# The bias row of a fused recurrence and MLP kernel: a matmul of ones against block transposes and a round trip through DRAM

## The chip, the cores and the metric

The kernel runs on one core of a Trainium2 chip. The metric is device time in microseconds (us); lower is better. The core's engines work side by side, each through its own list of instructions in order: TensorE (PE, with its weight loads shown as PEld), VectorE (DVE), ScalarE (ACT), GpSimd (POOL), and SyncE (SP), which here only issues DMAs. An instruction that waits for another engine or for a DMA holds everything behind it on its own engine.

## The reference

Two stages, joined. The first is a gated linear recurrence over 768 steps for 4 batches and 8 heads of width 48; its output is laid out as 3072 tokens of 384. The second is an MLP with a squared ReLU, a scale s and a bias b:

```
for t in range(S):
    state = alpha[:, :, t, :, None] * state + k[:, :, t] (x) v[:, :, t]
    y[:, :, t] = q[:, :, t] . state
x = y as [3072, 384]
r = max(x @ w_in, 0)              # w_in: 384 x 2048
g = s * (r * r) + b
out = g @ w_out                   # w_out: 2048 x 384
```

Since b is a single number, `g @ w_out` is `(r * r) @ (s * w_out)` plus one row that is the same for every token: b times the sum of each column of w_out. That row of 384 numbers is the **bias row**. The change is about how it is made.

## The kernel before, in words

The 3072 tokens are cut into 24 units of 128 (six units, n % 6 = 0 to 5, make one batch). For each unit the recurrence is done in chunk form. ACT takes the logarithm of alpha (`ln`, L239), PE sums it along the chunk (`cum_pe`, L255), ACT makes the two exponentials (`cum_act`, L268 and L269), DVE multiplies k and q by them (`kb_mul` L317, `qb_mul` L320), PE transposes both (`tr`, L328), and DVE copies the transposes to SBUF (`qk_copy`, L340). PE multiplies them into scores (`amat`, L361), DVE masks the scores (`mask`, L370), and PE makes the unit's output from scores and carried state (`y_pe`, L466 and L475). The state goes on through `t1` (DVE, L549) and `sd` (POOL, L559 and L563). The result is transposed for the MLP (`xt_pe` L527, `xt_act` L534). The MLP of a unit is four pieces u = 0 to 3: PE multiplies by w_in (`mp`, L573, 12 matmuls of 128 columns for each of four blocks, taken together by the trace), ACT applies the ReLU (`rl`, L586), DVE squares (`sq`, L593), PE multiplies by w_out (`o_pe`, L604). The sum of all four pieces stands in one bank of PSUM, `o_ps`.

Two places hold results back. Outputs of units 0 to 13 are parked in SBUF (`keep_sb`, which lies over the spent tile `w_in_st`); DVE adds the bias row to them later (`add_bias`, L655) and SP stores them. From unit 14 on, DVE adds the row while it empties `o_ps` (`o_out`, L621).

The bias row before is made so: DVE adds the sixteen 128-row blocks of the fp32 w_out (`w_out_st`) into `cs_sb` in seven additions of two blocks (`colsum`, L201 and L203), then one more (`bias_sum`, L206). Now `cs_sb[:, 0]` holds 128 partial sums for each of the 384 columns. `bias_row` multiplies a matrix of ones by it on PE, in fp32, into the PSUM bank `y_ps` (L209). That sums over the 128 partitions and puts the same row on all of them. ACT scales it by b into `bias_w` (L210).

The order of work is written out by hand. Each step is put at a position (`at(pos, ...)`), the list is sorted by position, and each engine gets its instructions in that order. From unit 10 on positions repeat with a period of 16 for two units, an even and an odd one, which take about 13.86 us, so one position is about 0.87 us. SP's DMAs go into one queue in the same order: for unit n a row of decays out to DRAM (`row_dr`, L304), the loads of unit n + 3 (L132), and the decays back, one number for each partition (`blast`, L311). SP waits for a semaphore before it issues a DMA, and the DMAs share eight completion semaphores in turn: the ninth DMA waits until the first has landed.

Names that the steps below use: `w_out_st` (the fp32 copy of w_out, no longer read once the column sums are done), `cs_sb`, `bias_w`, `y_ps`, `qkT` (the SBUF copy of the transposes), `sb_col` (s and b on every partition).

Of the kernel before, what the change touches and what calls it, by code (L numbers as in the profile page):

```python
# [8 lines left out]
FP32 = mybir.dt.float32  # L9
BF16 = mybir.dt.bfloat16  # L10
AF = mybir.ActivationFunctionType
ALU = mybir.AluOpType

@with_exitstack
def kernel(
# [12 lines left out]
    nc = tc.nc  # L28
# [6 lines left out]
    d_model = moe_w_in.shape[0]  # L35
# [13 lines left out]
    sb = ctx.enter_context(tc.tile_pool(name="sb", bufs=1))  # L49
    ps = ctx.enter_context(tc.tile_pool(name="ps", bufs=1, space=bass.MemoryType.PSUM))  # L50
    dr = ctx.enter_context(tc.tile_pool(name="dr", bufs=1, space=bass.MemoryType.DRAM))
# [5 lines left out]
    y_ps = ps.tile([128, 512], FP32, name="y_ps")  # L57
# [6 lines left out]
    def ring(name, shape, dtype, n):  # L64
        return [sb.tile(shape, dtype, name=f"{name}{i}") for i in range(n)]
# [12 lines left out]
    ones_f = sb.tile([128, 128], FP32, name="ones_f")  # L78
    sb_row = sb.tile([1, 2], FP32, name="sb_row")
    sb_col = sb.tile([128, 2], FP32, name="sb_col")  # L80
    s_col, b_col = sb_col[:, 0:1], sb_col[:, 1:2]
# [18 lines left out]
    qkT_p = qkT_all.rearrange("a u y -> a (u y)").rearrange("a (x p b s i) -> a x p b s i", x=2, p=NP, b=2, s=2)  # L100
    am_sb = [ring("am_a", [128, NP, 128], BF16, 2), ring("am_b", [128, NP, 128], BF16, 2)]
    blast = ring("blast", [128, NP, 1], FP32, 3)
    row_dr = [dr.tile([1, H * 48], FP32, name=f"row_dr{i}") for i in range(3)]
    t1_sb = sb.tile([128, NP, 96], FP32, name="t1_sb")
    sc_sb = sb.tile([128, NP, 96], FP32, name="sc_sb")
# [10 lines left out]
    w_out_st = sb.tile([128, NJ, d_model], FP32, name="w_out_st")  # L116
    w_out_bf = sb.tile([128, NJ, d_model], BF16, name="w_out_bf")
    cs_sb = sb.tile([128, 2, d_model], FP32, name="cs_sb")
    bias_w = sb.tile([128, d_model], FP32, name="bias_w")


    NKEEP = 14
# [82 lines left out]
    def bias_sum():  # L205
        nc.vector.tensor_tensor(out=cs_sb[:, 0], in0=cs_sb[:, 0], in1=cs_sb[:, 1], op=ALU.add)  # L206

    def bias_row():
        nc.tensor.matmul(out=y_ps[:, 0:384], lhsT=ones_f, rhs=cs_sb[:, 0], start=True, stop=True)  # L209
        nc.scalar.activation(out=bias_w, in_=y_ps[:, 0:384], func=AF.Copy, scale=b_col)  # L210

    def spread():
        nc.tensor.matmul(out=p_ps[:, 510:512], lhsT=ones_f[0:1], rhs=sb_row, start=True, stop=True)
# [286 lines left out]
    h0, h1, o, ct, a0, a1 = h_ps[0], h_ps[1], o_ps, ct_ps, *(a.rearrange("a p t -> a (p t)") for a in a_ps)  # L500
# [202 lines left out]
    for s in range(2):  # L703
        nc.vector.memset(mask_p[s], 0.0)
        for b in range(2):
            part = mask_p[s][64 * b : 64 * b + 64]
            nc.gpsimd.affine_select(
                out=part,
                in_=part,
# [17 lines left out]
    def at(pos, fn, *args):  # L727
        events.append((pos, len(events), fn, args))
# [55 lines left out]
    for i in range(3, 8):  # L784
        at(69.3 + 8 * (i - 3), colsum, i)
    at(103.3, bias_sum)
    at(105.5, bias_row)
    for n in range(NKEEP):
        at(125.3 + 4.55 * n, add_bias, n)
        at(126.2 + 4.55 * n, store, n, keep_sb[n])  # L790
# [15 lines left out]
    for n in range(4, NBLK):  # L806
        p = 8 * n
        f = max(0.0, min((n - 5) / 3.0, 1.0))
        c, t, a = 9.0 + 5.8 * f, 5.8 + 5.0 * f, 3.4 + 4.5 * f
# [59 lines left out]
```

## Time and profile before

| | us |
|---|---|
| three timed runs: median (lowest to highest) | 187.06 (186.27 to 187.86) |
| the execution that was profiled: its time | 185.68 |
| its span, first to last instruction | 183.9 |
| TensorE busy | 177.7 (97%) |
| VectorE busy | 143.4 (78%) |
| ScalarE busy | 122.6 (67%) |
| GpSimd busy | 60.3 (33%) |
| DMA data moved | 30.33 MB, mean 165 GB/s |

The profile is one execution. Its time is its span and 1.78 us around it, and it lies 1.38 us under the median of the timed runs. Busy times are sums of one engine's instructions over the whole span. TensorE's clock was granted in full throughout (1.000). Where the text says "at 119.14", it is the time in us from the start of the span. "Idle before, releaser" names what ended an engine's wait. Starts of matmuls in the timeline lie some tenths earlier than in the chain, since matmuls are pipelined.

### The profile page before, as it was taken

How to read it: one execution, taken by the hardware profiler on the slowest of the kernel's cores; microseconds unless marked ns; L12 is line 12 of the kernel's file. 1: busy time of each engine (PE TensorE's matmuls, PEld its weight loads, DVE VectorE, ACT ScalarE, POOL GpSimd, SP SyncE). 2: the span in 40 equal slices, each digit the busy share in tenths (PEclk: the TensorE clock that was granted, in tenths of full speed). 3: DMA queues.
4: the chain of work that ended last, by engine and by line, in shares of the span. 5: the costliest groups of instructions: out<-in, count | busy, mean ns of one | idle time of the engine just before them, and what ended most of it. 6: DMA issues, size and time to landing. Idle time of an engine off the chain costs nothing.

```text
span 183.9 us, 6223 instructions
## 1 busy us (share of the span) xinstructions
PE 177.7 (97%) x2506; PEld 142.3 (77%) x2506; DVE 143.4 (78%) x301; ACT 122.6 (67%) x253; POOL 60.3 (33%) x97
## 2 busy tenths in 40 slices
PE   7998999999999999999999999999999999999993
PEld 2565899866698687787888778878878878878793
DVE  7699879666657688987898976699789799886541
ACT  3888797985678956656766766846746746734750
POOL 7436471113230725042505343143103343333000
PEclk9999999999999999999999999999999999999999
DMA  6999999999188989982975564936895942214212
GB/s 156 315 324 359 235 295 385 255 213 207 16 166 169 188 173 177 172 174 41 169 140 121 105 125 92 192 63 145 171 201 139 211 133 92 73 59 157 60 52 77
DMA packets 105263, 30.33 MB, mean 165 GB/s; under 512 B 98436, under 2 KB 103699, under 8 KB 105235
## 3 DMA queue, kind: packets, MB, share of 16 engines
q1 hardware_dynamic: 105230, 29.94, 70.1%
q8 instruction: 19, 0.31, 0.7%
q14 instruction: 10, 0.07, 0.1%
q10 hardware_dynamic: 4, 0.00, 0.0%
HBM read 25.19 MB, written 4.74 MB: 163 GB/s over the span
## 4 chain that ended last, share of the span: by engine, by line
PE 90%; ACT 4%; DVE 3%; issue 1%; POOL 1%; ACTq 0%; POOLq 0%; DVEq 0%
PE h_ps L573 29%; PE o_ps L604 28%; PE ct_ps L328 5%; PE h_ps L604 3%; PE a_ps L573 2%; PE a_ps L361 2%; PE o_ps L229 2%; PE y_ps L475 2%; PE ct_ps L573 2%; PE h_ps L527 2%; PE ct_ps L255 2%; PE o_ps L573 2%; PE y_ps L466 1%; PE a_ps L630 1%; PE a_ps L604 1%; PE p_ps L488 1%
## 5 line engine op out<-in xcount | busy, mean ns | idle before, releaser
L573 PEld LDWEIGHTS <-w_in_bf 128*128 128x128 bf16 x1152 | 67.5, 98 | 5.1 <-DVE w_in_bf L176 0.9
L586 ACT ACTIVATE r_sb<-h_ps 128x512 bf16<-128x512 f32 x79 | 46.9, 603 | 30.7 <-PE h_ps L573 28.9
L604 PE MATMUL o_ps<-w_out_bf,gt_all 128*128 128x384 bf16 x320 | 64.0, 326 | 0.0
L573 PE MATMUL h_ps<-xd_all,w_in_bf 128*128 128x128 bf16 x948 | 60.3, 219 | 0.0
L559 POOL TENSOR_TENSOR sd_sb<-t_sb,blast 48x192 bf16<-48x192 f32 x40 | 26.9, 672 | 85.8 <-DVE t_sb L549 57.8
L593 DVE TENSOR_TENSOR gt_all<-r_sb 128x512 bf16<-128x512 bf16 x96 | 40.8, 442 | 16.5 <-ACT r_sb L586 16.3
L604 PEld LDWEIGHTS <-gt_all 128*128 128x128 bf16 x368 | 32.5, 98 | 15.6 <-issue 0.2
L250 POOL CAST v_bf<-v_sb 128x384 bf16<-128x384 f32 x23 | 15.4, 678 | 21.2 <-DMA v_sb<-in_v_dram 19.2
L317 DVE TENSOR_TENSOR kb_sb<-k_sb,bi_sb 128x384 bf16<-128x384 f32 x24 | 14.3, 595 | 7.1 <-ACT bi_sb L268 7.1
L534 ACT ACTIVATE xd_all<-h_ps 128x384 bf16<-128x384 bf16 x19 | 9.5, 502 | 8.6 <-PE h_ps L527 8.6
L320 DVE TENSOR_TENSOR qb_sb<-q_sb,b_sb 128x384 bf16<-128x384 f32 x24 | 13.5, 565 | 1.6 <-ACT b_sb L269 1.6
L563 POOL TENSOR_TENSOR sc_sb<-t_sb,blast 112x384 f32<-112x384 f32 x16 | 13.8, 864 | 1.3
L239 ACT ACTIVATE la_sb<-al_sb 128x384 bf16<-128x384 f32 x24 | 12.5, 529 | 2.6 <-DVE blast L720 2.3
L497 ACT ACTIVATE y_bf<-y_ps 128x384 bf16<-128x384 f32 x22 | 10.9, 497 | 3.5 <-PE y_ps L475 3.1
L340 DVE COPY qkT<-ct_ps 112x1024 bf16<-112x1024 bf16 x16 | 11.0, 686 | 2.3 <-PE ct_ps L328 2.1
L370 DVE TENSOR_TENSOR am_a<-a_ps,mask 128x512 bf16<-128x512 f32 x13 | 8.9, 688 | 4.4 <-PE a_ps L361 4.2
L328 PEld LDWEIGHTS <-qb_sb 128*112 128x112 bf16 x96 | 8.1, 130 | 3.4 <-DVE qb_sb L320 1.9
L268 ACT ACTIVATE bi_sb<-ct_ps 128x384 f32<-128x384 f32 x19 | 9.3, 489 | 2.1 <-PE ct_ps L255 1.9
L370 DVE TENSOR_TENSOR am_b<-a_ps,mask 128x512 bf16<-128x512 f32 x13 | 8.9, 684 | 1.7 <-PE a_ps L361 1.7
L269 ACT ACTIVATE b_sb<-ct_ps 128x384 f32<-128x384 f32 x19 | 9.4, 495 | 0.0
L655 DVE TENSOR_TENSOR w_in_st<-w_in_st,bias_w 128x384 f32<-128x384 f32 x14 | 8.3, 595 | 0.0
L328 PEld LDWEIGHTS <-kb_sb 128*112 128x112 bf16 x96 | 7.2, 130 | 0.7 <-DVE kb_sb L317 0.4
(142 smaller groups left out, 254.8 us busy)
## 6 DMA issues: line engine op xcount, KB each, us to landing
al_sb<-in_alpha_dram SPq DMA_DIRECT2D x20, 192.0 KB, 2.7
q_sb<-in_q_dram SPq DMA_DIRECT2D x20, 192.0 KB, 4.3
k_sb<-in_k_dram SPq DMA_DIRECT2D x20, 192.0 KB, 7.2
v_sb<-in_v_dram SPq DMA_DIRECT2D x20, 192.0 KB, 3.6
w_in_st<-in_moe_w_in_dram SPq DMA_DIRECT2D x4, 768.0 KB
w_out_st<-in_moe_w_out_dram SPq DMA_DIRECT2D x4, 768.0 KB
out_dram<-w_in_st SPq DMA_DIRECT2D x10, 192.0 KB
out_dram<-out_sb SPq DMA_DIRECT2D x5, 192.0 KB, 2.0
```

The costliest lines, as they stand in the source:

```text
L239: nc.scalar.activation(out=la_sb[n % 2][:, :, 0:48], in_=raw("al", n), func=AF.Ln)
L250: nc.gpsimd.tensor_copy(out=v_bf[n % 4], in_=raw("v", n))
L317: nc.vector.tensor_tensor(out=kb_sb[n % 4][:, :, 0:48], in0=raw("k", n), in1=bi_sb[n % 2], op=ALU.mult)
L320: nc.vector.tensor_tensor(out=qb_sb[n % 2][:, :, 0:48], in0=raw("q", n), in1=b_sb[n % 3], op=ALU.mult)
L328: nc.tensor.transpose(out=t_bank(n, x if n in pair_of else None)[0:112, x, p, :], in_=t.rearrange("a h d -> a (h d)")[:, 128 * p : 128 * p ...
L370: nc.vector.tensor_tensor(out=am_sb[e][n % 2], in0=a_bank(n)[e], in1=mask4, op=ALU.mult)
L559: nc.gpsimd.tensor_tensor(out=sd[r, :, d], in0=t1_sb[r, :, d], in1=bl[r].to_broadcast([48, NP, 48]), op=ALU.mult)
L563: nc.gpsimd.tensor_tensor(out=sc_sb[0:112], in0=t1_sb[0:112], in1=bl[0:112].to_broadcast([112, NP, 96]), op=ALU.mult)
L573: nc.tensor.matmul(out=hp[:, jj * C : (jj + 1) * C], lhsT=w_in_bf[:, kk, 128 * j : 128 * (j + 1)], rhs=xd_sb[n][:, kk], start=(kk == 0), s ...
L586: nc.scalar.activation(out=rs, in_=room((g, u)), func=AF.Relu)
L593: nc.vector.tensor_tensor(out=gt_sb[g][:, u * 512 : (u + 1) * 512], in0=rs, in1=rs, op=ALU.mult)
L604: nc.tensor.matmul(out=op[:, 0:d_model], lhsT=gt_sb[n][:, j * C : (j + 1) * C], rhs=w_out_bf[:, j, :], start=(j == 0), stop=(j == NJ - 1),)
```

## The change

The matmul of ones and the scaling on ACT are taken out. In their place:

- `bias_turn` (position 110.0), on DVE: `cs_sb[:, 0]` is transposed in blocks of 32 x 32 into `cs_sb[:, 1]`; then each partition of a group of 32 holds, for 12 columns of w_out, 32 partial sums side by side. A reduction sums each 32, so `part_sb` gets 12 numbers for each partition, and these are multiplied by b. Each of the four groups of 32 partitions now holds one partial bias row, scattered as 32 x 12.
- `bias_spread` (position 110.4), on SP: four small DMAs write the four partial rows to DRAM in the order of columns, 384 numbers of 4 bytes each; a fifth reads the four rows (6,144 bytes) back onto every one of the 128 partitions, into the first four blocks of `w_out_st` (786,432 bytes in all).
- `bias_add` (positions 120.5 and 123.5), on DVE: two additions make one row of the four, `bias_w`.

The additions of the bias to the parked outputs stay at positions 125.3 and on.

```diff
-    def bias_row():
-        nc.tensor.matmul(out=y_ps[:, 0:384], lhsT=ones_f, rhs=cs_sb[:, 0], start=True, stop=True)
-        nc.scalar.activation(out=bias_w, in_=y_ps[:, 0:384], func=AF.Copy, scale=b_col)
+    def bias_turn():
+
+        nc.vector.transpose(out=cs_sb[:, 1], in_=cs_sb[:, 0])
+        nc.vector.tensor_reduce(
+            out=part_sb, in_=cs_sb[:, 1].rearrange("a (b i) -> a b i", i=32), axis=mybir.AxisListType.X, op=ALU.add
+        )
+        nc.vector.tensor_scalar(out=part_sb, in0=part_sb, scalar1=b_col, scalar2=None, op0=ALU.mult)
+
+    def bias_spread():
+        for g in range(4):
+            nc.sync.dma_start(
+                out=bias_dr[g : g + 1].rearrange("o (b j) -> j (o b)", j=32), in_=part_sb[32 * g : 32 * g + 32]
+            )
+        nc.sync.dma_start(
+            out=w_out_st[:, 0:4].rearrange("a j m -> a (j m)"),
+            in_=bias_dr.rearrange("(o g) m -> o (g m)", o=1).to_broadcast((128, 4 * d_model)),
+        )
+
+    def bias_add(i):
+        if i == 0:
+            nc.vector.tensor_tensor(out=w_out_st[:, 0:2], in0=w_out_st[:, 0:2], in1=w_out_st[:, 2:4], op=ALU.add)
+        else:
+            nc.vector.tensor_tensor(out=bias_w, in0=w_out_st[:, 0], in1=w_out_st[:, 1], op=ALU.add)
...
     at(103.3, bias_sum)
-    at(105.5, bias_row)
+    at(110.0, bias_turn)
+    at(110.4, bias_spread)
+    at(120.5, bias_add, 0)
+    at(123.5, bias_add, 1)
```

More of the change, by code (lines that the diff above doesn't have):

```diff
@@ L102 @@
     blast = ring("blast", [128, NP, 1], FP32, 3)
+    bias_dr = dr.tile([4, d_model], FP32, name="bias_dr")
     row_dr = [dr.tile([1, H * 48], FP32, name=f"row_dr{i}") for i in range(3)]
@@ L119 @@
     bias_w = sb.tile([128, d_model], FP32, name="bias_w")
+    part_sb = sb.tile([128, d_model // 32], FP32, name="part_sb")
     NKEEP = 14
```

## The prediction

> **What bounds the kernel now.** I began with the page's chain of work that ended last, by engine:
>
> ```profile
> PE 90%; ACT 4%; DVE 3%; issue 1%; POOL 1%; ACTq 0%; POOLq 0%; DVEq 0%
> ```
>
> TensorE sets the end. In the windows of 1 us from 103 to 127 it is busy in every one, so what TensorE loses there nothing later makes good, and what it is spared the end gains. Next, the chain in order of time around the matmul that goes:
>
> ```profile
> 104.62 0.45 PE ct_ps L328 x8
> 105.07 0.70 PE y_ps L209 x2
> 105.77 0.65 PE o_ps L604 x4
> 106.42 0.17 PE h_ps L527 x3
> 106.59 0.33 PE a_ps L361 x8
> 106.92 0.05 PE y_ps L361
> ```
>
> The columns are start, length, engine, bank and line. The bias row costs TensorE 0.70 us of its chain (L209). Third, VectorE's timeline where the first new addition will stand, one period later:
>
> ```profile
> 118.37 0.85 DVE L593 TENSOR_TENSOR gt_all<-r_sb 128x512 bf16<-128x512 bf16 x2
> 119.14 0.55 DVE L549 TENSOR_TENSOR t_sb<-p_ps,sc_sb 112x384 f32<-112x384 f32 x1
> 119.67 0.69 DVE L340 COPY qkT<-ct_ps 112x1024 bf16<-112x1024 bf16 x1
> 120.81 0.69 DVE L370 TENSOR_TENSOR am_a<-a_ps,mask 128x512 bf16<-128x512 f32 x1 [0.45 <-PE a_ps L361]
> ```
>
> VectorE runs without a gap up to the copy of the odd unit's transposes (L340, done at 120.36). TensorE's odd scores, the matmuls into `y_ps` and `p_ps` (L361, at 120.78 in the chain), read that copy; this is where a late VectorE becomes a late TensorE.
>
> **Part 1, what goes.** The matmul: 0.70 us of chain. What is late next: the odd scores at 106.92 would move to 106.22, but their copy ends at 106.22 (start 105.54, 0.68), and 0.2 is lost there (at 120.78 the undelayed scores start 0.42 after the copy's end, of which I count some 0.25 as slack). I take 0.5 as the gain, bounds 0.25 and 0.7. ACT's scaling (L210, 0.58) stood before an idle stretch of 0.24 and after one of 1.23: nothing.
>
> **Part 2, bias_turn on VectorE.** It follows the first squaring at 109.35, so it starts at 109.35 + 0.33 (the spacing of squarings) - 0.5 = 109.2. No transpose or reduction stands in the trace. Nearest is the fp32 operation of 128x384, `bias_sum` L206, 0.54; the small one is 128x2, L214, 0.15. Two of the first and one of the second, with some 0.1 between dependent ones, make 1.35: done at about 110.55. Bounds: 0.3 each by the bf16 copy of 128x512 (L224, 0.28), 0.95 each by the 128x768 addition (L203); so 110.0 to 111.4. Behind it wait the second squaring (109.96) and `kb_mul` (111.21, itself waiting 0.82 for ACT). The squaring would end at 111.3; its matmul, like the one that reads the other squaring of the pair, comes after 111.9. `kb_mul` slips some 0.3, then `qb_mul`, whose transposes come at 113.40. Cost on the path: nothing; if the turn took 1 us more, some tenths.
>
> **Part 3, bias_spread on SP.** SP is idle from 107.4 to 111.59 and the DMA engines from 110 to 112.9, so nothing runs beside the writes at first. Four writes of 384 numbers of 4 bytes into DRAM are not in the trace. The nearest rows are `row_dr` (one piece of 1,536 bytes to DRAM) and `blast` (192 numbers of 4 bytes from DRAM):
>
> ```profile
> 147.69 0.25 SPq L304 DMA_DIRECT2D row_dr<-b_sb  x1
> 149.32 0.81 SPq L311 DMA_DIRECT2D blast<-row_dr  x2
> ```
>
> ```profile
> DMA to landing us min/median/max: 2.2/2.9/3.7
> ```
>
> `blast` waits for `row_dr`, so a write to DRAM is done 1.63 us after its issue begins (1.37 at 153.06). The second fence is `blast`'s own, from issue to landing. By the windows of half a microsecond its first data move about 0.93 us after 149.32, at 2 GB/s, which is 0.5 numbers per ns. At that pace four writes, 1,536 numbers, take 3.07 us. From 110.7: 0.93 + 3.07 + 0.5 (the rest of a write's 1.4) gives 115.2. Low end: only issue counts, 0.4 each as for `blast`, the last one 1.5 after its issue, 113.4. High end: half the pace, 118.3. I take 115.2.
>
> The fifth DMA waits on SP for all four. It moves 786,432 bytes. A store of 192 KB lands in 2.0 us, of which 0.5 is data at 380 GB/s (the stretch from 28 to 33, pieces of 1,536 bytes), so 1.5 is fixed. Data take 2.1 us at 380 GB/s and 3.35 at the 235 GB/s of the loads in 192-byte pieces: 3.6 to 4.85 after the issue. I take the middle, 4.25: the rows are there at **119.5**; ends 117.0 and 123.2.
>
> [...]
>
> Behind these five on SP stand `row_dr`, `blast` and the loads of units 19 and 20. They go out about 3.8 us later than at 111.59 and 115.82, the loads of unit 20 not before the broadcast has landed (they share its semaphore). Unit 19's alpha is read by the Ln at 125.77, and lands by about 123; `blast` by about 123 too, read at 126.98 by POOL; unit 20's alpha at 134.68. Hidden; with rows at 123.2 unit 19's alpha comes at about 126, and the Ln would wait some tenths in an ACT that is 67% busy.
>
> **Part 4, bias_add.** The first addition stands between the squarings (118.37) and `t1`, so VectorE reaches it at 119.14 - 0.5 = 118.64. Its own work is that of L203: 0.95, 0.87 as spacing. It puts the copy off by about 0.8; TensorE's slack there is 0.25, so the odd scores lose 0.55. POOL's state (L559 at 119.77, needed by L466 at 123.59) has room. The masks start 0.27 later, after an idle 0.45 is used up. The second addition (0.55, spacing 0.47) lies after the masks; it moves two squarings, an `o_out` and `kb_mul`, all of which end in time for a TensorE that is itself 0.55 late: nothing. To this comes the wait for the rows: 119.5 - 118.64 = 0.85, straight on through `t1`, copy and scores.
>
> **Sum.** -0.5 + 0.55 + 0.85 = +0.9 us; the profiled execution of 185.68 would become 186.6. Put on the median of 187.06, it is **187.9 us**.
>
> **Rivals.**
> 1. *The rows are there in time* (landing before 118.64). Then -0.5 + 0.55, with bounds -0.2 to +0.3: 187.1. For it: low ends of part 3. Without even the 0.55 the change would bring 0.7, the whole matmul, 186.4. That is less than 1%.
> 2. *The small writes are slow*: VectorE's wait becomes the bound, slower than before by over 1%. A gain or loss here is landing minus 118.6, so over 1% (1.87 us, which is about what a measurement of this kernel can tell from no change) begins at a landing of 120.5. Half the pace of `blast` puts it at 118.3 + 3.6 to 4.85 = 121.9 to 123.2: +3.3 to +4.6, 190.4 to 191.7. A pace of three quarters gives 120.5. Against it: the DMA engines have no other work then. For it: a write of scattered numbers is not a read, and neighbouring numbers come from different partitions.
> 3. *The broadcast is slow*: all 128 partitions read the same 6 KB. The slowest large row is the load of 384 KB at the start, 4.9 us to landing; twice that is 9.8, landing at 125.0: +6.4, 193.5. Against it, that row stood in a full queue.
>
> [...]
>
> 4. *The change does nothing*: the matmul was hidden. Against it, it is a link of the chain; its chance lies in rival 1.
>
> **Chances.** Forecast (a wait of 0 to 1.8): 0.46. Rival 1: 0.16. Rival 2: 0.28. Rival 3: 0.10. Faster by over 1% would need a gain of 1.87, where the matmul is 0.70: 0.02, out of rival 1. Within 1%: 0.46 + 0.14 = 0.60. Slower: 0.38. The range leaves out rival 3 and the far half of rival 2 above, and little below: 186.7 to 190.5.
>
> **What would show it.** TensorE without L209, one 0.70 us less; on VectorE three new operations of some 1.3 us in all at about 109.2; an idle gap ahead of the first addition, released by the DMA into `w_out_st`, of about 0.85; and the odd scores at about 121 late by 1.4 against their own run-up. Wrong it would be if the gap is over 2 us (then by which DMA), if there is none, or if a later stage is held by unit 19's loads.

## The result, and the profile after

| | before | after |
|---|---|---|
| timed runs side by side: median (lowest to highest), us | 186.44 (185.77 to 187.86) | 193.67 (193.02 to 194.57) |
| the execution that was profiled, us | 185.68 | 194.42 |
| its span, us | 183.9 | 192.6 |
| TensorE busy, us | 177.7 (97%) | 180.7 (94%) |
| mean granted TensorE clock | 1.000 | 0.973 |

After against before is 1.0386, with an interval of 1.0335 to 1.0436: the change makes the kernel 7.2 us slower. The prediction was 187.9 us, with a range up to 190.5.

The profiled execution of after had its clock halved from 18.7 to 22.1 us as well, long before the change acts; all that follows stands 1.40 us later than in the kernel before, and I take that off where I compare times with the prediction.

The page's chain by engine, for after:

```profile
PE 78%; DMA 7%; DVE 7%; ACT 4%; issue 2%; SPq 1%; ACTq 0%
```

DMAs, which were not in the chain before, are now 7% of it. To see where the time goes I use a landmark: the matmul that sums the logarithms of one unit (`cum_pe`), which comes once a unit and in the same place in both kernels. First before (starts in the first column, from TensorE's timeline), then after:

```profile
101.76 0.33 PE L255 MATMUL ct_ps<-la_sb,U_bf 128*128 128x384 bf16 x1
110.27 0.33 PE L255 MATMUL ct_ps<-la_sb,U_bf 128*128 128x384 bf16 x1
116.33 0.33 PE L255 MATMUL ct_ps<-la_sb,U_bf 128*128 128x384 bf16 x1
...
143.82 0.33 PE L255 MATMUL ct_ps<-la_sb,U_bf 128*128 128x384 bf16 x1
```

```profile
103.16 0.33 PE L277 MATMUL ct_ps<-la_sb,U_bf 128*128 128x384 bf16 x1
111.20 0.33 PE L277 MATMUL ct_ps<-la_sb,U_bf 128*128 128x384 bf16 x1
117.25 0.33 PE L277 MATMUL ct_ps<-la_sb,U_bf 128*128 128x384 bf16 x1
...
152.35 0.33 PE L277 MATMUL ct_ps<-la_sb,U_bf 128*128 128x384 bf16 x1
```

I call these A, B, C and D. From A to B, where the matmul of ones stood, after takes 8.04 against 8.51: **0.47 gained**. From B to C, where `bias_turn` stands, 6.05 against 6.06: nothing. From C to D 35.10 against 27.49: **7.61 lost**. Together +7.14, close to the difference of the medians (7.23). All of the loss lies between C and D, where `bias_add` stands. The chain in order of time there (start, length, what):

```profile
113.39 6.68 DMA bias_dr<-part_sb
...
120.21 4.89 DMA w_out_st<-bias_dr
...
125.11 0.07 DVE w_out_st L230
...
125.99 0.55 DVE t_sb L571
126.54 0.61 DVE qkT L362
...
127.81 1.39 PE o_ps L626 x4
129.20 2.43 PE h_ps L595 x24
```

Read it from the top: the last of the four small writes lands 6.68 us after it is issued; only then does the broadcast go out, and it takes 4.89; only then does the first addition run; behind it come `t1` and the copy of the transposes; and then TensorE's scores. VectorE's timeline shows the same from its side; the bracket gives its idle time and what ended it:

```profile
125.11 0.96 DVE L230 TENSOR_TENSOR w_out_st<-w_out_st 128x768 f32<-128x768 f32 x1 [4.56 <-DMA w_out_st<-bias_dr]
125.99 0.55 DVE L571 TENSOR_TENSOR t_sb<-p_ps,sc_sb 112x384 f32<-112x384 f32 x1
126.46 0.68 DVE L362 COPY qkT<-ct_ps 112x1024 bf16<-112x1024 bf16 x1
```

The last two lines of the chain hold a second thing. Four matmuls into `o_ps` take 1.39 and 24 into `h_ps` take 2.43; in the chain of before, at the same place, they take 0.76 and 1.34. Windows of half a microsecond show why (columns: window, its length, busy time of PE, PEld, DVE, ACT and POOL, then the granted clock, the DMA share, GB/s):

```profile
124.00:124.50 0.50, 0.00 (x0) 0.00 (x0) 0.00 (x0) 0.00 (x0) 0.00 (x0) 1.00 1.09 258
124.50:125.00 0.50, 0.00 (x0) 0.00 (x0) 0.00 (x0) 0.00 (x0) 0.00 (x0) 0.54 1.19 242
...
127.50:128.00 0.50, 0.50 (x7) 0.17 (x4) 0.50 (x2) 0.00 (x0) 0.42 (x2) 0.50 0.96 125
...
131.00:131.50 0.50, 0.50 (x9) 0.50 (x7) 0.29 (x1) 0.17 (x1) 0.00 (x0) 0.64 1.12 222
131.50:132.00 0.50, 0.50 (x7) 0.31 (x5) 0.50 (x2) 0.27 (x1) 0.00 (x0) 1.00 0.89 180
```

TensorE has nothing to do from about 121.7 to 127.2. At 124.5 its clock falls to a half, and it comes back only at 131.4, more than 4 us after work resumed.

### The profile page after: what moved, and what is told of

Same layout as the page of the kernel before. It is cut to its first block, busy times and chain, and to the rows that moved or that the text cites. A ratio compares the mean times of both kernels' runs of the same rounds, so it can differ in the third digit from the quotient of the medians.

```text
span 192.6 us, 6222 instructions
## 1 busy us (share of the span) xinstructions
PE 180.7 (94%) x2504; PEld 144.7 (75%) x2504; DVE 145.8 (76%) x306; ACT 122.1 (63%) x252; POOL 58.2 (30%) x97
## 4 chain that ended last, share of the span: by engine, by line
PE 78%; DMA 7%; DVE 7%; ACT 4%; issue 2%; SPq 1%; ACTq 0%
PE h_ps L595 24%; PE o_ps L626 23%; PE ct_ps L350 4%; DMA bias_dr<-part_sb 3%; PE h_ps L626 3%; DMA w_out_st<-bias_dr 3%; PE ct_ps L595 2%; PE o_ps L251 2%; PE o_ps L595 2%; PE a_ps L595 2%; PE a_ps L383 2%; PE y_ps L497 2%; DMA blast<-row_dr 1%; PE h_ps L549 1%; PE a_ps L652 1%
## 5 line engine op out<-in xcount | busy, mean ns | idle before, releaser
L595 PEld LDWEIGHTS <-w_in_bf 128*128 128x128 bf16 x1152 | 69.8, 100 | 5.3 <-DVE w_in_bf L178 0.9
L595 PE MATMUL h_ps<-xd_all,w_in_bf 128*128 128x128 bf16 x948 | 61.4, 221 | 0.0
L581 POOL TENSOR_TENSOR sd_sb<-t_sb,blast 48x192 bf16<-48x192 f32 x40 | 25.2, 630 | 94.8 <-DVE t_sb L571 59.7
L272 POOL CAST v_bf<-v_sb 128x384 bf16<-128x384 f32 x23 | 14.8, 652 | 22.9 <-DMA v_sb<-in_v_dram 20.8
L383 PEld LDWEIGHTS <-qkT 48*128 48x128 bf16 x160 | 4.6, 96 | 7.8 <-DVE qkT L362 5.9
```

Of the source, the lines that this page charges most:

```text
L272: nc.gpsimd.tensor_copy(out=v_bf[n % 4], in_=raw("v", n))
L581: nc.gpsimd.tensor_tensor(out=sd[r, :, d], in0=t1_sb[r, :, d], in1=bl[r].to_broadcast([48, NP, 48]), op=ALU.mult)
L595: nc.tensor.matmul(out=hp[:, jj * C : (jj + 1) * C], lhsT=w_in_bf[:, kk, 128 * j : 128 * (j + 1)], rhs=xd_sb[n][:, kk], start=(kk == 0), s ...
```

## The experiments

**Theory.** The four writes of scattered 4-byte numbers land late (6.68 us after the last issue); SP may not issue the broadcast before; VectorE waits for the broadcast (4.56 us) ahead of the copy that TensorE's odd scores need; TensorE stops (5.5 us), and the stop halves its clock (0.50). **Rivals:** what SP holds back meanwhile (loads of later units, the decays) sets the price; or it is the broadcast that is slow. Each expectation says itself what its theories A and B are. Ratios are to the kernel before, timed beside each.

### No wait for the rows

```diff
-            out=w_out_st[:, 0:4].rearrange("a j m -> a (j m)"),
+            out=w_out_st[:, 4:8].rearrange("a j m -> a (j m)"),
```

> The broadcast lands in the next four blocks of the spent w_out tile, so the two additions read old numbers and wait for no DMA; every instruction and every DMA stays. What is left out: the row that is added is not the bias row. Theory (the time went into VectorE's wait for the rows, 4.6 us, and into what follows from it, TensorE at half clock): about -0.5 for the matmul and +0.55 for the addition ahead of the copy, so 186.0 to 187.0 where the kernel before has 186.4, and a granted clock of 1.00 after 110. Rival (the late loads and state rows behind the spread in SP's queue hold a later stage): they are as late as in the changed kernel, so 189 or more.

Measured: 186.62 (186.18 to 187.07), ratio 1.0043 (1.0019 to 1.0066). SP's part of the waits (what is waited for, then us in all, times, longest) shows that it waits for the writes nearly as long as in after, where it is 6.2 us:

```profile
SPq L223 <- DMA bias_dr<-part_sb: 5.6, 1, 5.6
```

The granted clock is 1.000 over the whole span. With every DMA still there and only VectorE's wait gone, some 6.4 us of the loss are gone, by the ratios and from C to D (1.17 lost in place of 7.61). So what SP holds back is not the main price. It isn't quite free either: the next kernel, with fast writes, loses 0.60 from C to D. Half of the difference lies at the additions, which start 0.27 later. The other half lies some 16 us behind C: POOL waits 2.38 us for the v of a later unit, a load that went out behind the stalled SP. Its cast then falls beside VectorE's `kb_mul`, which takes 0.85 in place of 0.55. POOL's and VectorE's timelines:

```profile
131.84 0.80 POOL L272 CAST v_bf<-v_sb 128x384 bf16<-128x384 f32 x1 [2.38 <-DMA v_sb<-in_v_dram]
```

```profile
132.19 0.85 DVE L339 TENSOR_TENSOR kb_sb<-k_sb,bi_sb 128x384 bf16<-128x384 f32 x1
```

### Writes in pieces of 48 bytes

Each partition writes its 12 numbers side by side, and the second addition puts the columns in order while it reads.

```diff
-                out=bias_dr[g : g + 1].rearrange("o (b j) -> j (o b)", j=32), in_=part_sb[32 * g : 32 * g + 32]
+                out=bias_dr[g : g + 1].rearrange("o (j b) -> j (o b)", j=32), in_=part_sb[32 * g : 32 * g + 32]
...
-            nc.vector.tensor_tensor(out=bias_w, in0=w_out_st[:, 0], in1=w_out_st[:, 1], op=ALU.add)
+            rows = [w_out_st[:, x].rearrange("a (j b) -> a b j", j=32) for x in range(2)]
+            nc.vector.tensor_tensor(
+                out=bias_w.rearrange("a (b j) -> a b j", j=32), in0=rows[0], in1=rows[1], op=ALU.add
+            )
```

> The four small DMAs write each partition's 12 numbers side by side (48 bytes a piece, 32 pieces a DMA in place of 384), and the second addition reads the row in the permuted order, so the result is the same. Theory A (the 6.7 us from the last write's issue to its landing belong to the many 4-byte pieces): the writes land 1.5 to 2.5 us after the last issue, as the row of decays does (1.4 to 1.6), the broadcast goes out some 4 to 5 us earlier, VectorE waits 0 to 1 us, 186.5 to 188.0, no half clock. Theory B (a write to DRAM out of 32 partitions takes that long whatever its pieces, or the wait is the semaphore's): the landing stays at 6 to 7 us, and the time at 193 to 194.

Measured: 186.08 (185.82 to 186.56), ratio 1.0013 (0.9994 to 1.0031). SP's wait for the same number of bytes:

```profile
SPq L223 <- DMA bias_dr<-part_sb: 1.0, 1, 1.0
```

and VectorE's timeline, where the addition waits for nothing:

```profile
117.99 0.84 DVE L618 TENSOR_TENSOR gt_all<-r_sb 128x512 bf16<-128x512 bf16 x2
118.75 0.95 DVE L230 TENSOR_TENSOR w_out_st<-w_out_st 128x768 f32<-128x768 f32 x1
119.62 0.55 DVE L574 TENSOR_TENSOR t_sb<-p_ps,sc_sb 112x384 f32<-112x384 f32 x1
```

The time lies a little under the range of theory A, since VectorE doesn't wait at all. One edit, the order of the numbers in a 6 KB scratch row (with the addition that reads them), takes away the 7 us. A to B gains 0.48, C to D loses 0.60, which is the price of the addition itself where it stands.

### Four rows far apart, and 4-byte pieces with room between them

Here each 4-byte piece has 512 bytes to itself; a DMA fills the gaps beforehand, and the broadcast reads the four rows from places 196,608 bytes apart.

```diff
-    bias_dr = dr.tile([4, d_model], FP32, name="bias_dr")
+    bias_dr = dr.tile([4, d_model, 128], FP32, name="bias_dr")
...
-                out=bias_dr[g : g + 1].rearrange("o (b j) -> j (o b)", j=32), in_=part_sb[32 * g : 32 * g + 32]
+                out=bias_dr[g, :, 0:1].rearrange("(b j) o -> j (b o)", j=32), in_=part_sb[32 * g : 32 * g + 32]
...
-            out=w_out_st[:, 0:4].rearrange("a j m -> a (j m)"),
-            in_=bias_dr.rearrange("(o g) m -> o (g m)", o=1).to_broadcast((128, 4 * d_model)),
+            out=w_out_st[:, 0:4],
+            in_=bias_dr[:, 0:3].rearrange("(o g) r c -> o g (r c)", o=1).to_broadcast((128, 4, d_model)),
...
```

> The 4-byte pieces stay 1,536, but each goes to a place of its own, 512 bytes from the next, in place of 32 neighbours in 128 bytes. One small DMA fills the stretch that the broadcast reads; the row that is added is not the bias row. Theory A1 (neighbouring pieces from different partitions hold one another up in memory): the writes land 2 to 3 us after the last issue, as the decays read in 4-byte pieces do (2.2 to 3.7), and the time falls under 190. Theory A2 (each small write has its price wherever it goes): the landing stays at 6 to 7 us and the time at 193 or more.

Measured, in one run: 191.18. The writes came a little sooner than theory A1 had them, and yet the time did not fall under 190. The chain says both:

```profile
111.78 1.75 DMA bias_dr<-part_sb
113.68 8.55 DMA w_out_st<-bias_dr
```

1,536 pieces of 4 bytes, the same number as in after, land in 1.75 us after the last issue in place of 6.68; so neither the number nor the size of the pieces alone is the cause; it matters where they lie. The broadcast, on the other hand, now takes 8.55. That was new, and the next two runs are about it: pieces of 48 bytes again, with the four rows once as far apart as here, and once 2,048 bytes apart.

```diff
-    bias_dr = dr.tile([4, d_model], FP32, name="bias_dr")
+    bias_dr = dr.tile([4, d_model, 128], FP32, name="bias_dr")
...
-                out=bias_dr[g : g + 1].rearrange("o (j b) -> j (o b)", j=32), in_=part_sb[32 * g : 32 * g + 32]
+                out=bias_dr[g, 0:3].rearrange("r c -> (r c)").rearrange("(j b) -> j b", j=32), in_=part_sb[32 * g : 32 * g + 32]
...
```

> Writes of 48-byte pieces, side by side, as in the fast variant, but the four partial rows stand 196,608 bytes apart, as in the variant with spaced 4-byte pieces. It tells what made that one's broadcast take 8.55 us. If the distance or the pieces of 1,536 bytes did: the writes land 1 to 2 us after the last issue, the broadcast takes 7.5 to 9 us again, VectorE waits 2.5 to 4 us: 189 to 191. If it was the spaced small pieces just written there: the broadcast takes 4.5 to 5.5 us, VectorE waits under 0.5: 185.8 to 187.

Measured, in one run: 191.67, a little above the 189 to 191 (TensorE's clock halved here too, see the last section). The writes take 1.42 in the chain; the broadcast:

```profile
113.69 8.08 DMA w_out_st<-bias_dr
```

```diff
-    bias_dr = dr.tile([4, d_model], FP32, name="bias_dr")
+    bias_dr = dr.tile([4, 512], FP32, name="bias_dr")
...
```

> As the variant with the four rows 196,608 bytes apart, but with the rows 2,048 bytes apart: the broadcast still reads four pieces of 1,536 bytes for each partition, all out of 8 KB. If the distance made the broadcast slow (8.0 us there): 4.5 to 5.5 us here, VectorE waits under 0.5, 185.8 to 187. If the four pieces in place of one of 6,144 bytes did: 7.5 to 8.5 us, VectorE waits 2.5 to 3.5, 189 to 192.

Measured, in one run: 186.31. The issue of the broadcast begins at 113.75, and VectorE's addition does not wait for it:

```profile
118.95 0.95 DVE L230 TENSOR_TENSOR w_out_st<-w_out_st 128x768 f32<-128x768 f32 x1
```

So, counted from the start of its issue as in the chains, it took at most 5.2 us; the last count on its semaphore in the trace stands at 118.26, which makes 4.5. The four pieces of 1,536 bytes cost nothing (in after, with one stretch of 6,144, it took 4.89); with 196,608 bytes from row to row it took 8.08. Why the distance matters when all partitions read the same four rows stays open.

### What makes the writes slow

Two runs measure the writes alone: 4-byte pieces with 4 bytes between them whose neighbours come from the same partition, and 4-byte pieces in the scattered order (neighbours from different partitions) that are 64 bytes apart.

```diff
-    bias_dr = dr.tile([4, d_model], FP32, name="bias_dr")
+    bias_dr = dr.tile([4, d_model, 2], FP32, name="bias_dr")
...
-                out=bias_dr[g : g + 1].rearrange("o (b j) -> j (o b)", j=32), in_=part_sb[32 * g : 32 * g + 32]
+                out=bias_dr[g, :, 0:1].rearrange("(j b) o -> j (b o)", j=32), in_=part_sb[32 * g : 32 * g + 32]
...
```

> It measures the writes alone: pieces of 4 bytes with 4 bytes between them, but neighbouring pieces come from the same partition; a small DMA reads some of it back into one partition and the additions take old numbers, so the row added isn't the bias row and nothing waits for it on VectorE: time 185.8 to 187.2, as without the wait. If 4-byte pieces close together are what is slow, whoever writes them: SP waits 5 to 6.5 us for the writes, as with the scattered order. [...]

```diff
-    bias_dr = dr.tile([4, d_model], FP32, name="bias_dr")
+    bias_dr = dr.tile([4, d_model, 16], FP32, name="bias_dr")
...
-                out=bias_dr[g : g + 1].rearrange("o (b j) -> j (o b)", j=32), in_=part_sb[32 * g : 32 * g + 32]
+                out=bias_dr[g, :, 0:1].rearrange("(b j) o -> j (b o)", j=32), in_=part_sb[32 * g : 32 * g + 32]
...
```

> It measures the writes alone too: 4-byte pieces in the scattered order, neighbours out of different partitions, but 64 bytes apart in place of 4 (512 bytes apart took 1.3 us of SP's wait). A small DMA reads some of it back and the additions take old numbers; the row added isn't the bias row: 185.8 to 187.2. If pieces collide only within the same 64 bytes: SP waits 1 to 2 us. If they collide within the same 512 bytes: 4 to 6.5 us.

Measured, in one run each: 186.52 and 186.01. SP's wait, first with the 8-byte pitch, then with 64:

```profile
SPq L229 <- DMA bias_dr<-part_sb: 5.2, 1, 5.2
```

```profile
SPq L229 <- DMA bias_dr<-part_sb: 1.5, 1, 1.5
```

Put in order, SP's wait for 1,536 numbers of 4 bytes:

| pieces | pieces in one stretch of 64 bytes | SP waits, us |
|---|---|---|
| 4 bytes, 4 apart, neighbours from other partitions (after) | 16 | 6.2; 5.6 to 5.9 in the four other kernels with these writes |
| 4 bytes, 8 apart, neighbours mostly from the same partition | 8 | 5.2 |
| 4 bytes, 64 apart, neighbours from other partitions | 1 | 1.5 |
| 4 bytes, 512 apart, neighbours from other partitions | 1 | 1.3 |
| 48 bytes, side by side | 2, in part | 1.0 |

With 8 or 16 of the 4-byte pieces in 64 bytes SP waited 5.2 us (neighbours mostly from the same partition) or 5.6 to 6.2 (from others); with one of them there, or with pieces of 48 bytes, 1.0 to 1.5. Where between 8 and 64 bytes the change lies was not tried, and no run shows what makes it.

### TensorE kept at work while it waits

22 matmuls on data of no use, ahead of the odd scores, with the writes of after:

```diff
+    at(122.3, busy, 22, ("y", 0))
```

> Twenty-two matmuls of ones (128x512, some 0.21 us each, 4.7 us in all) into an idle bank stand ahead of the odd scores that wait for VectorE; nothing else is changed and no result of theirs is used. Theory (TensorE's standing still for over 5 us brings the half clock, and the half clock some 2.1 us): the clock stays at 1.00, the copy of the transposes is as late as before, and the time falls by 1.5 to 2.2, to 191.5 to 192.2. Rival (the clock falls for another reason, or costs nothing since VectorE or ACT would be the bound then): 193 to 194 or more.

Measured: 190.70 (190.50 to 194.05), ratio 1.025 (1.0202 to 1.0298), against 1.0386: about 2.5 us less by the ratios, more than the 1.5 to 2.2 that was expected. The profiled execution is that of 194.05: its clock was halved from 14.3 to 24.6 us, long before the change acts, which puts C at 119.05, and it was 1.00 from 28 to 188 us, through the wait and behind it. VectorE still waits for the rows; TensorE's four matmuls behind the odd scores take what they take in before (0.82, at 120.94 there; 1.46 in after):

```profile
126.27 0.96 DVE L230 TENSOR_TENSOR w_out_st<-w_out_st 128x768 f32<-128x768 f32 x1 [3.82 <-DMA w_out_st<-bias_dr]
```

```profile
128.68 0.82 PE L626 MATMUL o_ps<-w_out_bf,gt_all 128*128 128x384 bf16 x4
```

From C to D it loses 5.03 in place of 7.61. Of these 2.58, 0.64 come from an addition that starts sooner (4.41 us late against 5.05, by the table further on); the other 1.9 go with the clock, at 1.00 here and 0.50 in after.

### The additions behind the masks

The DMAs as in after; the first addition stands 2.2 positions later and the second 0.7 earlier, right behind the first.

```diff
-    at(120.5, bias_add, 0)
-    at(123.5, bias_add, 1)
+    at(122.7, bias_add, 0)
+    at(122.8, bias_add, 1)
```

> The two additions stand after the odd unit's two masks instead of between the squarings; the writes are the slow, scattered ones. The rows land as late as before, at about 123.7 in the frame of the kernel before, and VectorE comes to the addition at about 122. Theory A (the price is the place of the wait: ahead of the copy that the odd scores need, it stops TensorE, and the stop halves its clock): VectorE waits 1 to 2.5 us, TensorE has the scores and the work behind them in hand, no idle stretch of it is over 2.5 us, the granted clock is 1.00 in undisturbed runs; the late squarings cost 1 to 3 us: 187.5 to 189.5. Theory B (the late DMAs themselves, or what SP holds back behind them, set the price): 192 or more, as with the additions in their old place.

Measured: 186.76 (186.14 to 187.23), ratio 1.0040 (1.0013 to 1.0066), better than theory A had it. The writes land as late as ever, but VectorE copies the transposes and masks the scores first, and then waits little:

```profile
122.97 0.96 DVE L230 TENSOR_TENSOR w_out_st<-w_out_st 128x768 f32<-128x768 f32 x1 [0.45 <-DMA w_out_st<-bias_dr]
```

TensorE loses nothing at the odd scores (C to the next landmark 7.81 against 7.80) and then 1.16 us in one place, where `o_out` comes late behind the two additions; another 0.3 goes some 16 us behind C, where POOL waits 1.88 us for a late v. The clock stays at 1.00:

```profile
126.18 0.81 PE L626 MATMUL o_ps<-w_out_bf,gt_all 128*128 128x384 bf16 x4 [1.16 <-DVE out_sb L643]
```

So most of what the slow writes cost, some 6.4 us by the ratios, is the price of the place where VectorE waited for them. The wait was 0.45 and not 1 to 2.5 us: in the frame of before (A lies 0.31 earlier here) VectorE came to the addition at 122.83, some 0.8 us later than I had it, and the rows were there at 123.25, half a microsecond sooner.

### All of it earlier

The column sums, the turn and the DMAs stand 8 to 14 positions earlier (in the traces the turn comes 8 to 9 us earlier, the DMAs 7 to 8), the additions in a gap of VectorE; first with the scattered writes, then with pieces of 48 bytes.

```diff
-        at(69.3 + 8 * (i - 3), colsum, i)
-    at(103.3, bias_sum)
-    at(110.0, bias_turn)
-    at(110.4, bias_spread)
-    at(120.5, bias_add, 0)
-    at(123.5, bias_add, 1)
+        at((61.3, 69.3, 77.3, 85.3, 87.3)[i - 3], colsum, i)
+    at(93.3, bias_sum)
+    at(101.3, bias_turn)
+    at(101.7, bias_spread)
+    at(117.4, bias_add, 0)
+    at(117.5, bias_add, 1)
```

> The scattered writes as they are, but the column sums, the turn and the five DMAs some 8 to 10 positions earlier (7 to 8 us), and the additions at 117.4 and 117.5, before the even masks' period ends. Theory A (slow writes cost only while somebody waits for the rows): the writes still take over 5 us after their last issue and SP waits some 6 us for them, but the rows land at about 115 to 117, VectorE waits at most 1 us for them, TensorE keeps its clock: 185.8 to 187.3. Theory B (a stalled SP costs by itself, since the loads of unit 18 and the decays' round trip stand behind it): Ln or the multiplication on POOL waits for a DMA, 188 or more.

Measured: 186.46 (185.47 to 187.76), ratio 1.0019 (0.9983 to 1.0056). VectorE waits in a place where it has time:

```profile
115.19 1.25 DVE L230 TENSOR_TENSOR w_out_st<-w_out_st 128x768 f32<-128x768 f32 x1 [0.99 <-DMA w_out_st<-bias_dr]
```

> The early positions and, in addition, pieces of 48 bytes in place of 4. Rows at about 110, no wait anywhere; the additions stand where VectorE has idle time, so that of the gain of 0.47 at the matmul less than 0.3 is given back: 185.2 to 186.1, ratio 0.997 to 1.000. If the early column sums cost as much as they save: 186.0 to 186.5.

Measured: 185.93 (185.42 to 189.15), ratio 0.9994 (0.9965 to 1.0022): no better than before, so the hoped-for gain did not come. The landmarks say why. In both kernels A to B takes 7.81 against 8.51, the whole 0.70 of the matmul, and with 48-byte pieces C to D loses nothing. But the stretch ahead of A, from the landmark at 88.22 before to that at 95.71, takes 8.2 in both against 7.49: the column sum that now stands at 90.88, ahead of a copy of transposes, costs 0.73. VectorE's work was moved from in front of one copy to in front of another.

## Why the prediction was wrong, point by point

**Part 1, the matmul: right.** 0.5 foreseen, 0.47 measured (0.46 to 0.48 wherever the turn stayed in its place). The reason holds too: what is late next is the copy of the odd transposes. Where that copy also came earlier, because `bias_sum` no longer stood before it, the whole 0.70 came through.

**Part 2, the turn: right.** VectorE's timeline of after:

```profile
110.56 0.57 DVE L212 STREAM_TRANSPOSE cs_sb<-cs_sb 128x384 f32<-128x384 f32 x1
111.17 0.55 DVE L213 TENSOR_REDUCE part_sb<-cs_sb 128x12 f32<-128x384 f32 x1
111.76 0.23 DVE L216 TENSOR_SCALAR part_sb<-part_sb,sb_col 128x12 f32<-128x12 f32 x1
```

Some 1.4 us with the gaps, against 1.35, and no cost from B to C.

**Part 3, the spread: here it failed, in the last term of "0.93 + 3.07 + 0.5 (the rest of a write's 1.4) gives 115.2".** Times are with 1.40 taken off: the first issue came at 110.62 (110.7 foreseen). The writes landed at 118.67, 8.05 us after the first issue in place of 4.5, just beyond the high end (118.3). The pace, which was read off `blast`, was not what failed. Data begin to move 0.7 us after the first issue (0.93 foreseen) and move for about 2.0 us (3.07 foreseen). Then nothing moves at all until SP's wait for them ends: this rest took 5.3 us where 0.5 was foreseen. In the trace's own time, data move from 112.75 to 114.75 and the wait ends at 120.07; the counts on the semaphores of all four writes come in singly from 114.97 on (window, length, PE, PEld, DVE, ACT, POOL, clock, DMA share, GB/s):

```profile
113.00:114.00 1.00, 1.00 (x10) 0.66 (x8) 1.00 (x4) 1.00 (x3) 0.00 (x0) 1.00 0.35 3
114.00:115.00 1.00, 1.00 (x14) 0.83 (x12) 0.58 (x3) 0.25 (x1) 0.79 (x2) 1.00 0.29 2
115.00:116.00 1.00, 1.00 (x17) 0.87 (x16) 0.50 (x1) 0.00 (x0) 0.92 (x2) 1.00 0.00 0
...
119.00:120.00 1.00, 1.00 (x20) 0.77 (x17) 0.72 (x2) 0.69 (x3) 0.00 (x0) 1.00 0.00 0
```

So rival 2 was right that "a write of scattered numbers is not a read". But the price is in the landing and not in the pace, and neighbours from different partitions, the other half of its reason, are not needed for it (5.2 us where they mostly come from the same one).

The broadcast took 4.89, at the upper end (4.85) and not the middle. So the rows were there at 123.7 where 119.5 was foreseen: 3.55 of it from the writes and 0.64 from the broadcast.

**Part 3, later loads "hidden": nearly.** With VectorE's wait gone, the late v of a later unit cost 0.3. In after TensorE is itself so late that it doesn't show.

**Part 4, the addition: right, and the wait's place too.** 0.55 foreseen, 0.60 measured where there was no wait. The wait goes "straight on through t1, copy and scores", as written.

**The sum: one term was missing, the clock.** I charged TensorE for the time it stands still and not for what follows. The four kernels with a wait at that place close with it. Columns: what C to D loses; the addition's own 0.60 and how much later it starts than in the variant of 48 bytes without a wait (2.81 us behind C); and, as an estimate of what the half clock cost, half of the time that TensorE worked at it, read from its windows (at a clock of 0.50 the chain had 1.39 and 2.43 us in place of 0.76 and 1.34):

| | loss C to D | 0.60 + late start | half of the slow stretch | left over |
|---|---|---|---|---|
| after | 7.61 | 5.65 | 4.16 / 2 = 2.08 | -0.12 |
| 48 bytes, rows far apart | 6.02 | 3.51 | 5.33 / 2 = 2.67 | -0.16 |
| 4 bytes, 512 apart | 6.08 | 4.43 | 3.42 / 2 = 1.71 | -0.06 |
| TensorE kept at work | 5.03 | 5.01 | 0 | 0.02 |

For after: -0.47 from the matmul, +0.60 from the addition, +5.05 from the rows, +1.96 that goes with the clock: +7.14. The forecast had -0.5, +0.55 and +0.85. Of the miss of 6.2 the rows make 4.2 and the clock 2.0.

**The rivals.** Rival 2 was the right one, with a landing of 121.9 to 123.2 and 190.4 to 191.7; the landing was half a microsecond later still, and its price lacked the clock. Rival 3 gave the nearest time, 193.5, by luck: it made the broadcast 9.8 us, and it took 4.89. Rival 1 is the kernel with 48-byte pieces: 187.1 on a median of 187.06, no change, and so it was (1.0013).

## What to carry to other kernels

When a small scatter goes to DRAM, lay each partition's numbers out side by side and let a later engine read them in the other order (SP waited 1.0 us here in place of 6.2); and price a write by the landing of a write, not by the pace of a read of the same shape (5.3 us of landing where 0.5 was foreseen). When a new wait may be long, ask what stands behind it in the queue: with the same late rows the kernel was 7.2 us slower where they were waited for ahead of the copy that TensorE needs, and 0.7 us slower (ratio 1.0040) where the wait came behind it. Where TensorE may stop, charge for a half clock too: at this place of the kernel a stop of 1.2 us did not bring it, and stops of 3.3, 4.3 and 5.5 did, at an estimated 2.7, 1.7 and 2.1 us. That gives no limit: near the start, where TensorE's work has gaps, the half clock came in after with a stop of 0.5 us, and in the profiled execution with TensorE kept at work, where no wait of TensorE was longer than 1.3.

## What the runs showed of the hardware that was not expected

- **4-byte writes 4 or 8 bytes apart landed late, in after with no data moving.** See the table of pitches: 5.2 to 6.2 us of waiting at 4 and 8 bytes, 1.3 to 1.5 at 64 and 512. In after, 5.3 us pass between the last data and the end of the wait, with a DMA share of 0.00 from 115 to 120.
- **A broadcast of four rows 196,608 bytes apart took 8.1 to 8.6 us**, where rows within 8 KB took at most 5.2 (4.89 in after, with the rows side by side). No run shows what slows it.
- **The half clock lasted 3.4, 6.8 or 10.2 us, and not in step with the stop.** A window's mean clock gives the moment of the change: 0.54 from 124.50 on means 124.54, and 0.64 from 131.00 on means 131.36, so 6.82 us in after. With the rows far apart, 122.38 to 129.21, 6.83 us:

```profile
122.00:122.50 0.50, 0.00 (x0) 0.00 (x0) 0.50 (x1) 0.00 (x0) 0.00 (x0) 0.88 0.95 191
...
129.00:129.50 0.50, 0.50 (x7) 0.27 (x6) 0.33 (x1) 0.13 (x1) 0.00 (x0) 0.79 0.85 168
```

With 4-byte pieces 512 apart, 124.85 to 128.27, 3.42 us:

```profile
124.50:125.00 0.50, 0.50 (x10) 0.30 (x6) 0.50 (x2) 0.00 (x0) 0.42 (x2) 0.85 0.97 184
...
128.00:128.50 0.50, 0.50 (x8) 0.43 (x6) 0.50 (x2) 0.00 (x0) 0.00 (x0) 0.73 1.16 234
```

So the price does not go with the length of the stop: a stop of 3.3 us (120.5 to 123.9) cost 2.7 us of clock, and one of 4.3 us (120.1 to 124.3) cost 1.7. Nor does the moment of the fall: with the rows far apart the clock fell 1.8 us after TensorE's last work, in after 2.8, and with the pieces 512 apart 4.8, half a microsecond behind the end of the stop. Two stretches lie before the change acts: 18.72 to 22.14 in after (3.42 us), and 14.31 to 24.55 in the execution with TensorE kept at work (10.24 us). TensorE was not idle throughout ahead of these falls: with the rows far apart it had worked for 1.57 of the last 3.41 us, and at 18.72 in after for 2.72 of the last 3.42. How much work keeps the full clock was not tried, and no run shows what sets the three lengths.
